# A gated mix of two long convolutions: P rows in two buffers, one reader per PSUM tile, and a new written-out order

## The chip, the cores and the metric

The kernel runs on one core of one Trainium2 chip. The metric is the device time of one execution in microseconds (us), lower is better. Several runs of the kernel are timed, and their median stands for it. The profile is taken from one further execution.

The engines are named as in the profile: PE is TensorE (matrix products into PSUM), PEld its loading of weights, DVE is VectorE, ACT is ScalarE, POOL is GpSimd and SP is SyncE. SP issues most transfers, POOL and ACT some.

## The reference

Both branches take the same input x (1 x 2048 x 448, bf16). Branch A is a long convolution of x with a kernel K that is built from 256 complex modes for each of 448 channels; branch B convolves a 4-tap convolution of k, times v, with a given kernel ssm_k, and multiplies by x. A gate for each time step mixes them:

```
g = sigmoid((x * gate_w).sum(-1, keepdims=True))
# A
logdA = exp(log_dt)[:, None] * (A_re + 1j * A_im)
P = exp(logdA[:, :, None] * l[None, None, :])          # 448 x 256 x 2048, complex
K = einsum("dn,dnl,dn->dl", C, P, dt * B).real
a = irfft(rfft(pad(x)) * rfft(pad(K)))[:2048] + x * Dskip
# B
kv = shift_conv(k, shift_k) * v                        # 4 taps
b = x * (irfft(rfft(pad(kv)) * rfft(pad(ssm_k)))[:2048] + kv * ssm_D)
return g * a + (1 - g) * b
```

## The kernel before, in words

**Layout.** The 448 channels are 4 groups of 112. The work is cut into four chunks H of 28 channels per group (NQG = 4, NC = 28), and each chunk of K into two blocks j (NBLK = 8 blocks of CB = 14 channels per group, M = 112 channels in a block over both halves of the modes and all groups).

**The long convolutions** are transforms by matrix products. For one chunk of one signal, spread_in multiplies the columns by Wc into PSUM tiles (ps_c in the profile), which ScalarE copies to a tile zs; transform multiplies by W2 (s_W in the profile; PSUM tile ps) and copies back; swapped makes a second tile zsS with the two halves of the partitions exchanged, by DMA; products multiplies the two by the transform of the other signal on VectorE. Stage a multiplies by R (sa_R; PSUM tiles ps_a, result U) and stage b by G (sb_G; PSUM tiles ps_b), and an epilogue takes ps_b. These tiles of 7168 bytes in each partition (zs, zsS, zsK, U, some of the early ones) share a ring with the tag "q" of NBQ = 7 buffers: a new tile takes the buffer of the one seven before it, and its first writer waits for that one's last reader.

**The kernel K** (class KGen, line 408) is a product of two tables of powers, Q rows (32, tile kg_TQ, for two blocks at once: q_rows, line 426) and P rows (32, tile kg_TP, for one block), multiplied by TensorE into a PSUM bank pk (224 matmuls for a block). Both come from ET (EQ and EP), powers at a few levels, by products of complex numbers on VectorE: mult (line 414) writes four products into a tile kg_P4 (kg_P in the profile), add (line 423) sums them in pairs. In block (line 458) the first 8 of the leading 16 P rows are made so. Rows 8 to 15 are two multiplications, one into kg_P4 and one into rows 8 to 15 themselves, and a DMA from GpSimd's queue that adds the first onto the second (accum_op). back then makes the 16 mirrored rows from the leading 16 in two instructions (128x1792), rows 8 to 15 of the mirrored ones first: kg_TP <- kg_TP, ET in the profile. ScalarE copies pk to S (kg_S), and gather (line 502) sorts S into KT (kg_KT) by matmuls with selecting matrices (PSUM tiles ps_g); spread puts KT into the tile zsK of the chunk (KA).

**The exponents** (class Tables, line 542): the products dt * A (real and imaginary) and the coefficients B * C stand in one tile hold for each half of the modes, with three planes for each block; save (line 595) writes what later chunks need to DRAM in two DMAs, and levels (line 611) loads them for chunk H. For each level VectorE makes a phase (ks_ph), ScalarE its sine (ET <- ks_ph) and the exponential of the real part (ks_mag), VectorE multiplies them; ScalarE makes a negated copy of parts of EQ (ET <- ET), 12 instructions in all. Sine and exponential need different tables on ScalarE, loaded by an ACT_TABLE_LOAD at each change between them.

**The other operations the change touches.** sk_cols (line 738) adds ssm_D to the first column of ssm_k's chunk on GpSimd, ahead of spread_in. transform_half (line 354) transforms half a chunk's zsK at the end: two PSUM tiles of two banks, 16 matmuls each, with two copies by two engines (evac_two, line 715, lets ScalarE and VectorE alternate).

**The sequence.** body (line 675) does the setup and the first chunk of B, then step (line 939) for blocks 0 to 6, each with one chunk of A or B; then the tail (lines 988 to 1009): the last chunk of A's signal, B's last chunk, block 7, mix (line 924), and the halves of the last convolution.

**The order.** All these calls are not issued where they stand: the class Order records them with numbers, and issue (line 148) lays them out as the string ORDER (lines 42 to 111) lists them, with a dependency from each instruction to the one before it on the same engine. So each engine's order is written out by hand, every instruction has the line L148 in the profile, and groups are told apart by tile names.

Of the kernel before, what the change touches and what calls it, by code (L numbers as in the profile page):

```python
# [10 lines left out]
ALU = mybir.AluOpType  # L11
f32 = mybir.dt.float32
# [5 lines left out]
P = 128  # L18
# [8 lines left out]
M = 8 * CB  # L27
# [11 lines left out]
NBQ = 7  # L39
# [3 lines left out]
    "0-1 540 2 945 947 23 886 559 533 553-554 896-897 560 31 13 544 538 542-543 967 36 946 539 546 549 60 12 551 22 "  # L43
    "561 563 565 569 955 562 8 970 566 61 953-954 25 62-68 572-580 831 934 931 928 529 3 930 938 7 564 53 34-35 557 "
    "601-605 568 606-609 32 582-589 33 30 531 962 541 545 548 581 4 9 17 29 936 958 591 914 905 44 889 907 550 887 "
    "941 590 874 851 878 527-528 11 555 850 864 968 956 926 833 556 619-623 929 830 592-599 860 863 924 855 28 927 "
    "829 600 843 859 836 835 834 610-614 14 24 839 948 898-899 949 877 530 942 842 837 950 832 933 838 27 615-617 "
    "932 923 957 879 16 624-627 618 854 847 873 960 861 963 875 628 865 868 26 20 70 41 848 631 535 844-845 18 880 "
    "567 532 840 849 906 964 69 630 470-497 19 937 629 299-326 925 888 883 558 959 876 852-853 916 185-212 915 866 "
    "856-857 965 858 890 869-870 547 891 882 862 867 908 1500 498-525 42 900 570 871 917 885 918 872 327-354 841 971 "  # L50
    "213-240 43 961 966 881 355 55 552 241 10 15 5 21 6 951 526 356-411 58 939 534 536 38 242-297 884 128-155 57 56 "
    "943 412 909 846 39 952 537 298 2873 2887 2883 40 571 2884 46 413-440 1478 2885 441-469 2896 37 54 632 935 "
    "156-184 2888 71-98 2895 2877 99-127 910 892 921 913 2878 911 2876 940 912 1480 47 684-692 893 920 903 650-666 "
    "633-648 667-679 919 680-682 649 683 765-771 895 772-781 1479 2882 48 45 748-764 711-719 731-737 720-727 738-746 "
    "728 782-789 894 969 747 1151-1164 790 1483 1165-1166 901 904 1125-1140 1486 922 1481 1167 902 49 51 1142-1150 "
    "1141 791-799 693-701 1491 1202-1209 702-710 944 1108-1124 1482 2874 1502 1210 1168-1181 1501 1182-1183 "
    "1091-1103 1484 1503 1104-1106 52 50 1184-1191 1107 809-816 1489 1192-1200 817 800-807 1201 59 972-1001 1504 "
    "1271-1278 808 1002-1016 1279 1490 1505 2875 1298-1305 1487 1017-1031 1306 1506 1032-1046 1493 1307-1315 1507 "
    "1047-1061 818-826 1494 1508 1062-1084 2880 1316-1323 1495 729 1085-1086 1324 1492 2563-2569 1325-1333 2570-2578 "
    "1496 2579 1485 1883-1890 1499 1891 1849-1862 1488 1498 1476 1497 2879 1510 1863-1864 2881 1334-1342 730 2889 "  # L60
    "1509 1511 1280-1287 1289-1296 1512-1543 1865 1297 2897 1544-1639 1473 828 1640-1703 2900 1704-1735 1288 2899 "
    "2901 827 2118-2119 2904 1736 2905-2906 2120 1245-1261 2909 2121 2908 2910 2919 2122 2918 2123 1228-1244 "
    "1262-1269 2892 1270 2920 2124 2886 1211-1218 1474 2893 2126 1475 2125 2890 1219-1227 2911 2128 1477 2922 "
    "2537-2544 1755-1794 2545 2902 2520-2535 1795 1408-1439 2907 2536 2486-2502 2898 2894 2503-2519 2903 1440-1455 "
    "1828 1456-1471 2923 1737-1753 2924 1343-1358 2912 2921 1359-1390 2914 2913 1391-1406 1472 2127 1754 1866-1872 "
    "2915 2891 1829 2946 2928 2927 2129 2937 1814-1821 2969 2943 1873-1879 2938 2934-2935 2933 2666-2673 2929 2674 "
    "2916-2917 2940 1407 2930 1880-1882 2925 2130-2161 1831 2162-2193 1830 2194-2225 1832-1845 2675-2682 1846-1848 "
    "2683 2947 2944 2226-2353 2948 2971 1909-1916 1822 2949 2932 1823-1826 2354 2926 2970 1827 1952-1960 2945 2941 "
    "1805-1812 1943-1951 2693-2701 1917-1925 2931 2952 1892-1907 1926-1941 2942 2972 1813 1942 2936 2955 1908 "
    "2546-2552 2973 2553-2561 4620-4626 2958 2974 1796-1803 2959 4627-4628 2684-2691 2597-2604 2975 2939 2562 2605 "  # L70
    "1804 2692 2580-2595 2962 2950 2373-2413 1961-1968 1970-1977 2596 1969 1978 2711-2718 2355-2371 2702-2709 2719 "
    "4145 4153 2720-2727 2963 2951 2961 2053-2068 2710 2069-2116 2964 2976 2965 2372 2977 2728 2979 4149 2729-2737 "
    "2432-2439 4152 2440 2968 2953 1988-2019 2966 4148 4151 4147 2960 2954 2020-2035 4186 4150 3298 2117 2423-2431 "
    "2956 2967 2036-2051 2978 3318-3324 2980 4146 2957 4176 3352-3359 4154 3360 2981-3044 4177 3587 4185 4187 3297 "
    "3045-3076 3300 3299 2441-2444 3077-3108 4167 2445 4178 2870 3325-3334 4168 1979-1987 4169 2414-2422 3109-3172 "
    "4160 4159 4161 3173-3205 2466-2473 2052 4180 3589 3588 2474 3361-3368 4165 4164 4166 3412-3420 3590 3395-3402 "
    "4181-4182 3591 4170 4155 3592-3593 3403-3410 3369-3376 3378-3385 3411 3386-3393 3377 2457-2464 3394 4156-4157 "
    "3301-3314 4191 4190 3335-3341 2446 3342-3350 3315-3316 2465 3224-3263 4192 3594-3595 3522-3553 3317 3554-3569 "
    "4200 3570-3585 3351 4162 2475-2482 3597 3264 4158 4179 2483 4193 4188 3596 4195 4194 4196 3457-3488 3206-3222 "
    "3586 3223 3489-3520 4163 4171 3274-3281 4172-4173 2448-2455 4183 4199 3282 5892-5899 3283-3290 4197 2456 3598 "  # L80
    "5900 4205 4203 1087 4204 4209 4212 3599-3630 3430-3437 2447 4184 4218 3521 4213 3631-3662 2868 4202 2871 4241 "
    "3421-3428 3663-3726 4215 4174 4214 4175 3727-3822 4216 3429 3823 4217 2869 2485 2484 2640-2647 4201 3291 4211 "
    "3438 4242-4243 3292-3295 2648-2655 3296 4219 2656 4220-4221 2657-2665 4244 4206 4224 3265-3272 4245 3439-3447 "
    "4198 2623-2639 4227 2606-2613 4210 3273 4189 4208 4222 3448-3455 4246 4207 5415 4223 2872 5050-5062 4247 4230 "
    "4249 3842-3882 4226 3824-3840 4248 4250 3456 2614-2621 4233 3841 3901-3908 4231 4225 5063-5065 4234 2622 5066 "
    "5442 4586-4592 5067-5079 4235 5080-5082 3909 5083 4593-4602 2803-2834 5441 5422 5424 5423 5093-5099 4232 4251 "
    "4236 2835-2866 1088 4237 5417 2738-2769 4228 5421 4240 4229 2867 5429 5419-5420 5100-5108 4239 3915 2770-2801 "
    "5127-5140 4252 5141-5142 5418 4238 4665 5109 5143 3892-3900 2802 5416 5084-5091 5443 5033-5048 3910-3913 "
    "5430-5431 5446-5447 5437-5438 4569-4575 3914 5432 5448-5449 5426 5439 4576-4584 5049 4253-4316 1090 4317-4444 "
    "5425 4445-4476 5455 5444 5427 5092 5222-5229 5434 5456 4667 5435 4585 5457 4666 5436 4668 5144-5150 4669 5458 "  # L90
    "5151 4670-4671 3883-3890 4672-4673 5230 5875-5881 5470 5882-5890 5450 4675 5451 5152 3891 3917-3924 3944-3951 "
    "5891 5110-5123 4477 5469 3952 1089 5124-5125 3925 5126 5472 5428 5471 5461 3926-3934 5452-5453 5240-5247 "
    "3935-3942 4478-4494 5213-5220 3943 5221 5460 5462 4603-4616 5248 5440 5276-5283 5464 4617-4618 5231-5238 5454 "
    "5511 5465 3916 5463 5459 5433 4674 4676-4772 3954 5466 5445 5489 5467 4495 5476 5284 4773-4804 5482 5239 "
    "4805-4836 5487 4837-4868 3953 4869-4900 5490 4619 3972-3987 5491 5512 5494 5513 5478 5473 4496-4535 3989-3996 "
    "5497 5481 5492 3997-4004 5468 3988 3955-3962 4005-4013 3963-3970 4536 5493 4014 4656-4663 5514 5499 5837 "
    "4546-4553 5496 5515 5500 5498 5484 3971 4554 4664 5841-5854 5516 5258-5266 5855-5856 5501 5838 4564-4568 "
    "5267-5275 5475 4555-4563 4629-4637 4901 5517 4638-4645 5504 4537-4544 5488 4080-4095 4545 4646 4096-4111 "
    "4920-4960 5519 5485 4902-4918 5505 5483 5518 5858-5871 4919 4970-4977 5872-5873 5857 5506 4978 5474 5480 5486 "
    "4112-4143 5477 4015-4030 5502 4961-4969 4144 5507 5479 4031-4078 4979-4986 4079 5495 4987 5503 5510 5249-5256 "  # L100
# [251 lines left out]


def transform_half(nc, psum, W, zs, evac, half):
    for kk in range(2):
        pt = psum.tile([P, 2, 512], f32, name="ps_2", tag="ps")
        for i in range(16):
            k = 16 * kk + i
# [686 lines left out]
```

## Time and profile before

| | before |
|---|---|
| median of 3 runs | 277.68 us (277.12 to 280.39) |
| profiled execution | 277.69 us, of which the span is 275.8 us |
| TensorE: matmuls, weight loads | 210.7 us (76% of the span), 193.3 us (70%) |
| VectorE | 241.7 us (88%), 488 instructions |
| ScalarE | 226.7 us (82%), 383 instructions |
| GpSimd | 15.9 us (6%), 51 instructions |
| mean granted TensorE clock | 0.956 |
| accumulate DMA kg_TP <- kg_P | 8 issues of 448 KB, 5.7 us to landing (median) |
| ScalarE's table loads | 11, 1283 ns each |

How to read it: the span is the profiled stretch from the first instruction to the last, and 1.9 us of the execution lie around it. A row for a group of instructions gives its engine, operation, output <- inputs, shape and count, then its busy time and the mean of one, then how long the engine was idle just ahead of them and what ended that. A row of the waits gives the waiting engine and tile, what it waited for, and the total, number and longest of the waits. A row of the timeline gives start, duration, and in brackets the idle time before it. Instructions of one engine overlap somewhat, so that the time from start to start is shorter than the duration.

### The profile page before, as it was taken

The page shows a single profiled execution, that of the slowest core. Times are in us where ns is not written, and L with a number is a line of the kernel's source. Part 1 is how long each engine was busy: PE and PEld are TensorE (multiplying, and loading weights), DVE is VectorE, ACT ScalarE, POOL GpSimd, SP SyncE. Part 2 cuts the span into 40 slices and gives each one's busy share as a digit, 9 for nine tenths or more (in the row PEclk, how much of TensorE's full clock was granted, in tenths as well). Part 3 has the DMA queues.
Part 4 walks back from the last instruction along what each step waited for, and adds up shares of the span by engine and source line. Part 5 has one row for each costly group of instructions (what it writes and reads, how often), then busy time and mean ns, then how long its engine had stood idle before and what let it go on. Part 6 is the DMA issues. An engine that isn't in the chain of part 4 may idle for free.

```text
span 275.8 us, 12739 instructions
## 1 busy us (share of the span) xinstructions
PE 210.7 (76%) x5770; PEld 193.3 (70%) x5770; DVE 241.7 (88%) x488; ACT 226.7 (82%) x383; POOL 15.9 (6%) x51
## 2 busy tenths in 40 slices
PE   0610958879988799798997789867887999699830
PEld 0500858877887798687995779766886899688820
DVE  7599899999989799979996899899999997967950
ACT  2795696999899999998998799999999989546400
POOL 8000000000400000100010001001001001000000
PEclk9999999999999899998998999999999999979975
DMA  7999799607804500390093019003042263600077
GB/s 149 224 204 172 131 235 175 99 1 153 118 5 91 116 5 4 83 186 5 5 209 47 5 50 199 10 2 70 6 90 64 54 138 60 147 5 2 2 141 127
DMA packets 55110, 24.74 MB, mean 90 GB/s; under 512 B 49680, under 2 KB 52368, under 8 KB 55056
## 3 DMA queue, kind: packets, MB, share of 16 engines
q1 hardware_dynamic: 48640, 19.34, 37.7%
q0 software_dynamic: 1152, 3.67, 7.2%
q10 hardware_dynamic: 5264, 0.92, 2.1%
q8 instruction: 45, 0.74, 1.2%
q14 instruction: 9, 0.07, 0.1%
HBM read 7.95 MB, written 2.87 MB: 39 GB/s over the span
## 4 chain that ended last, share of the span: by engine, by line
ACT 38%; PE 29%; DVE 15%; DMA 9%; issue 5%; SPq 0%; DVEq 0%; POOL 0%; POOLq 0%; ACTq 0%
ACT zs L148 15%; ACT ET L148 7%; ACT U L148 6%; DMA kg_TP<-kg_P 6%; PE pk L148 5%; PE ps_a L148 5%; PE ps L148 5%; PE ps_c L148 5%; PE ps_b L148 5%; ACT zsK L148 5%; DVE vt L148 2%; DVE scratch L148 2%; PE ps_g L148 2%; PE ps_gate L148 2%; DMA skraw<-in_B_ssm_k_dram 2%
## 5 line engine op out<-in xcount | busy, mean ns | idle before, releaser
L148 ACT CAST zs<-ps 128x896 bf16<-128x896 f32 x48 | 44.0, 944 | 1.0 <-PE ps L148 0.6
L148 ACT CAST zs<-ps_c 128x1024 bf16<-128x1024 f32 (+1 forms) x48 | 42.7, 937 | 1.3 <-PE ps_c L148 1.2
L148 PEld LDWEIGHTS <-front 128*32 128x32 bf16 (+1 forms) x496 | 19.1, 159 | 27.3 <-issue 22.3
L148 PEld LDWEIGHTS <-s_W 128*128 128x128 bf16 x544 | 28.9, 100 | 12.7 <-issue 9.6
L148 PE MATMUL pk<-kg_TP,kg_TQ 128*32 128x32 bf16 x1792 | 33.2, 242 | 5.1 <-issue 2.9
L148 PEld LDWEIGHTS <-kg_TQ 128*32 128x32 bf16 x1792 | 31.2, 160 | 7.0 <-issue 4.8
L148 PE MATMUL ps_a<-sa_R,zs 128*128 128x128 bf16 x224 | 32.7, 235 | 0.3
L148 ACT CAST U<-ps_a 128x1024 bf16<-128x1024 f32 (+1 forms) x30 | 27.2, 936 | 6.9 <-PE ps_a L148 6.7
L148 PE MATMUL ps_b<-U,sb_G 128*128 128x28 bf16 x1024 | 29.5, 175 | 4.1 <-issue 1.4
L148 PE MATMUL ps_a<-sa_R,zsS 128*128 128x128 bf16 x224 | 32.1, 232 | 0.5 <-DVE zsS L148 0.5
L148 PE MATMUL ps<-zs,s_W 128*128 128x112 bf16 x384 | 27.7, 220 | 5.5 <-ACT zs L148 4.2
L148 PEld LDWEIGHTS <-sb_G 128*128 128x128 bf16 x1024 | 27.8, 96 | 5.8 <-issue 3.2
L148 DVE TENSOR_TENSOR kg_TP<-kg_TP,ET 128x1792 bf16<-128x1792 bf16 x24 | 26.1, 1090 | 5.8 <-DMA kg_TP<-kg_P 5.0
L148 PEld LDWEIGHTS <-zsS 128*128 128x128 bf16 x224 | 29.6, 152 | 1.3 <-DVE zsS L148 0.7
L148 PEld LDWEIGHTS <-zs 128*128 128x128 bf16 x224 | 29.4, 151 | 0.8
L148 PE MATMUL ps_v<-front 128*32 128x336 bf16 (+3 forms) x448 | 16.0, 310 | 16.0 <-DVE front L148 13.1
L148 ACT ACTIVATE ET<-ks_ph 128x448 bf16<-128x448 int16 x40 | 23.2, 602 | 4.1 <-DVE kg_P L148 2.6
L148 DVE TENSOR_TENSOR kg_TQ<-kg_TQ,ET 128x896 bf16<-128x896 bf16 (+1 forms) x36 | 24.8, 730 | 0.0
L148 DVE TENSOR_TENSOR kg_P<-kg_TP,ET 128x1792 bf16<-128x1792 bf16 (+1 forms) x24 | 22.4, 934 | 0.1
L148 PE MATMUL ps_c<-Wc,uu 128*64 128x128 bf16 x224 | 18.4, 290 | 1.6 <-ACT U L148 0.6
L148 PE MATMUL ps_c<-Wc,vt 128*64 128x128 bf16 x224 | 17.1, 285 | 1.4 <-ACT zs L148 1.2
L148 PEld LDWEIGHTS <-uu 128*64 128x64 bf16 x224 | 16.5, 210 | 2.4 <-issue 1.5
(102 smaller groups left out, 427.4 us busy)
## 6 DMA issues: line engine op xcount, KB each, us to landing
zsS<-zs SPq DMA_DIRECT2D x16, 448.0 KB, 5.7
kg_TP<-kg_P POOLq DMA_DIRECT2D x8, 448.0 KB, 5.7
vt<-in_B_v_dram SPq DMA_DIRECT2D x4, 448.0 KB, 6.8
skraw<-in_B_ssm_k_dram SPq DMA_DIRECT2D x16, 112.0 KB, 4.8
uu<-in_A_u_dram SPq DMA_DIRECT2D x4, 448.0 KB, 8.5
ks_xf<-xfd SPq DMA_DIRECT2D x3, 336.0 KB, 3.3
out_dram<-vt ACTq DMA_DIRECT2D x8, 112.0 KB, 3.8
out_dram<-vt SPq DMA_DIRECT2D x8, 112.0 KB, 3.6
```

Source lines behind the costliest of these rows:

```text
L148: ins = f(*args, **kw)
```

## The change: what it does, and the diff

- **P rows.** One tile TA of 48 rows is allocated once in place of a tile of 32 rows for each block. Even blocks have their leading 16 rows at 0 to 15, odd ones at 32 to 47, and the mirrored rows of both are 16 to 31. TensorE's operand for pk spans the mirrored rows and the block's own leading ones; for odd blocks the halves come in the other sequence, so that S is rotated by 16 rows, and gather splits selections that wrap around (16 matmuls more in all). The tile is 7168 bytes a partition larger, and NBQ goes from 7 to 6.
- **Rows 8 to 15 of block 7** are made by two mult and add pairs of four rows each in place of the two multiplications and the accumulate DMA. The other blocks keep the DMA (in a function summed).
- **Exponents and coefficients** are held in three separate parts for each half of the modes in place of three planes of one tile; save writes six DMAs in place of two.
- **The 12 negations of Q** go from ScalarE to VectorE, the 4 additions of sk_cols from GpSimd to VectorE.
- **transform_half** uses four PSUM tiles of one bank, 8 matmuls and one copy each.
- **ORDER** is new throughout. The number of recorded calls goes from 6758 to 6779.

```diff
-NBQ = 7
+NBQ = 6
...
 def transform_half(nc, psum, W, zs, evac, half):
-    for kk in range(2):
-        pt = psum.tile([P, 2, 512], f32, name="ps_2", tag="ps")
-        for i in range(16):
-            k = 16 * kk + i
-            nc.tensor.matmul(pt[:, i // 8, (i % 8) * 56:(i % 8 + 1) * 56], lhsT=W[:, k].rearrange("p r s -> p (r s)"),
-                             rhs=half_of(zs, k, k + 1, half), start=True, stop=True)
-        for i in range(2):
-            k0 = 16 * kk + 8 * i
-            evac(half_of(zs, k0, k0 + 8, half), pt[:, i, 0:448].rearrange("p (k c) -> p k c", c=CB), i)
+    for kk in range(4):
+        pt = psum.tile([P, 512], f32, name="ps_2", tag="ps")
+        for i in range(8):
+            nc.tensor.matmul(pt[:, i * 56:(i + 1) * 56], lhsT=W[:, 8 * kk + i].rearrange("p r s -> p (r s)"),
+                             rhs=half_of(zs, 8 * kk + i, 8 * kk + i + 1, half), start=True, stop=True)
+        evac(half_of(zs, 8 * kk, 8 * kk + 8, half), pt[:, 0:448].rearrange("p (k c) -> p k c", c=CB), kk % 2)
...
+    def summed(self, dst, src, r, m):
+        n = src.shape[1]
+        part = self.pool.tile([P, 8 * 2 * M], bf16, name="kg_P4", tag="kg_P4", bufs=2)[:, 0:n * 2 * m]
+        for c, out in enumerate((part.rearrange("p (n v m) -> p n v m", n=n, v=2), dst)):
+            self.nc.vector.tensor_tensor(out=out, in0=src[:, :, c].unsqueeze(2).to_broadcast([P, n, 2, m]),
+                                         in1=bass.AP(r.tensor, r.offset + c * m, [list(r.ap[0]), [0, n], [-m, 2], [1, m]]), op=ALU.mult)
+        self.nc.gpsimd.dma_start(dst.rearrange("p n v m -> p (n v m)"), part, accum_op=ALU.add)
...
-        TP = self.pool.tile([P, 32, 2, M], bf16, name="kg_TP")
+        if j == 0:
+            self.TA = self.pool.tile([P, 48, 2, M], bf16, name="kg_TP")
+        TP, late = self.TA[:, 32 * (j % 2):32 * (j % 2) + 16], self.TA[:, 16:32]
+        both = self.TA[:, 16 * (j % 2):16 * (j % 2) + 32]
...
-            V.tensor_tensor(out=TP[:, 16 + i0:16 + i1], in0=src,
+            V.tensor_tensor(out=late[:, i0:i1], in0=src,
...
+        if j == NBLK - 1:
+            add(8, mult(TP[:, 0:4], 64))
+            add(12, mult(TP[:, 4:8], 64))
+        else:
+            self.summed(TP[:, 8:16], TP[:, 0:8], EP[:, entry_of(64) - EQ_N + 1], M)
...
-                        r0 = TP[:, 0, c, m:m + 1]
-                        rhs = bass.AP(r0.tensor, r0.offset, [list(r0.ap[0]), [32 * M + (1 - 2 * c) * M, 2], [2 * M, 16]])
+                        d = c ^ (j % 2)
+                        r0 = both[:, 0, d, m:m + 1]
+                        rhs = bass.AP(r0.tensor, r0.offset, [list(r0.ap[0]), [32 * M + (1 - 2 * d) * M, 2], [2 * M, 16]])
...
-        self.hold = [early[:, 4096 + 1344 * i:5440 + 1344 * i].bitcast(f32).rearrange("p (b t m) -> p b t m", b=4, t=3) for i in range(2)]
+        part = lambda i, t: early[:, 4096 + 1344 * i + 448 * t:4544 + 1344 * i + 448 * t].bitcast(f32).rearrange("p (b m) -> p b m", b=4)
+        self.hold = [[part(i, t) for t in range(3)] for i in range(2)]
...
-            self.dma.dma_start(self.xfd[:, 4 * i + b:4 * i + 4], t[:, b:4])
+            for k in range(3):
+                self.dma.dma_start(self.xfd[:, 4 * i + b:4 * i + 4, k], t[k][:, b:4])
...
-                    nc.scalar.mul(B[:, :, 2], B[:, :, 0], -1.0)
+                    V.tensor_scalar(out=B[:, :, 2], in0=B[:, :, 0], scalar1=-1.0, scalar2=None, op0=ALU.mult)
...
-        nc.gpsimd.tensor_tensor(out=raw[:, :, 0], in0=raw[:, :, 0], in1=dB[:, H * NC:(H + 1) * NC], op=ALU.add)
+        V.tensor_tensor(out=raw[:, :, 0], in0=raw[:, :, 0], in1=dB[:, H * NC:(H + 1) * NC], op=ALU.add)
```

## The prediction, made before the changed kernel ran

> **What bounds the kernel now.** I read the totals and the chain first, then the waits of VectorE, the windows, and the last 40 us instruction by instruction.
>
> ```profile
> span 275.8 us, 12739 instructions
> PE 210.7 (76%) x5770; PEld 193.3 (70%) x5770; DVE 241.7 (88%) x488; ACT 226.7 (82%) x383; POOL 15.9 (6%) x51
> ACT 38%; PE 29%; DVE 15%; DMA 9%; issue 5%; SPq 0%; DVEq 0%; POOL 0%; POOLq 0%; ACTq 0%
> ```
>
> VectorE (DVE) has the longest list, and the chain of work that ended last passes between ScalarE (ACT), TensorE (PE) and VectorE: no engine alone sets the end. The windows say where each does:
>
> ```profile
> 140.00:160.00 20.00, 16.47 (x507) 14.89 (x494) 16.70 (x34) 17.11 (x35) 1.01 (x2) 0.91 0.36 67
> 160.00:180.00 20.00, 17.27 (x553) 16.15 (x553) 19.14 (x39) 19.73 (x36) 0.86 (x1) 1.00 0.40 89
> 180.00:200.00 20.00, 15.79 (x471) 14.53 (x464) 18.99 (x42) 19.97 (x33) 0.85 (x1) 1.00 0.14 27
> 200.00:220.00 20.00, 16.98 (x444) 15.39 (x435) 19.50 (x32) 19.86 (x38) 0.85 (x1) 1.00 0.34 72
> 240.00:250.00 10.00, 9.80 (x314) 8.92 (x307) 6.56 (x9) 3.96 (x7) 0.00 (x0) 0.83 0.02 5
> ```
>
> (Stretch, length, busy time of PE, weight loads, VectorE, ScalarE, GpSimd, clock, DMA.) From 140 to 160 both VectorE and ScalarE sit idle for some 3 us; from 160 to 220 ScalarE is 99% busy and VectorE 96%; from 240 to 250 TensorE is the bound. VectorE's waits:
>
> ```profile
> DVE kg_TP L148 <- DMA kg_TP<-kg_P: 5.0, 3, 2.1
> DVE kg_KT L148 <- PE ps_g L148: 3.4, 1, 3.4
> DVE ks_ph L148 <- ACT ET L148: 3.1, 5, 1.1
> DVE ks_ph L148 <- ACT early L148: 3.0, 1, 3.0
> DVE zsS L148 <- ACT zsK L148: 2.7, 2, 1.9
> DVE kg_TP L148 <- PE pk L148: 1.4, 2, 0.8
> ```
>
> The first is the accumulate DMA ahead of the mirrored rows; the sixth is P rows that may not be overwritten before pk's matmuls have read the last block's.
>
> **The sum's base.** The profiled execution took 277.69 us for a span of 275.8; the median of the three runs is 277.68, so both are the same base. All terms below are on VectorE's path up to the last row of block 7, then on the tail's path behind that row.
>
> **VectorE gets work: +2.7.** Twelve negations come from ScalarE. The like row is 274 ns an instruction (TENSOR_SCALAR ET<-ET, 128x448), 0.19 us from start to start (158.61 to 158.80): 8 x 0.19 and 4 half as wide at 0.13 make 2.0; by full durations it is 3.0 at most, and 0 if they fill idle time. Four sk adds from GpSimd are 28 elements a lane; the nearest row (128x64, start to start 148.36 to 148.52) gives 0.16, I take 0.1 each, 0.4. Block 7 has two adds in place of its DMA: 128x896, 0.62 us each, 0.54 start to start, 1.1. That is 3.5 in all. Over the new list up to and with the last row instruction, the same durations sum to 220.3 where they summed to 217.6: 2.7, the rest of the 3.5 is offset by work now listed behind it. No cover is claimed.
>
> **Waits for P rows go: -6.4.** With two buffers the leading rows of a block are written while TensorE still reads the other block's: the 1.4 goes, since the mirrored rows shared by both come last in a block. The accumulate DMA takes 5.7 us from issue to landing (median; 4.3 to 8.2) and in the new list has 7 to 18 us of VectorE work between its multiplications and its reader, where it had about 5: the 5.0 goes. What is late next is ScalarE's activation for ks_ph, below. If that cover shrank to the old 5 us, the old rate would come back, 5.0 over 8 DMAs, 0.6 for each of the 7 left, 4.4; if a DMA took the longest landing, 8.2, the shortest cover falls short by 1.2.
>
> **ScalarE gets lighter: -2.0.** Twelve negations cost it 5.1 + 1.8 us of rows:
>
> ```profile
> L148 ACT ACTIVATE ET<-ET 128x448 bf16<-128x448 bf16 x8 | 5.1, 638 | 1.0 <-DVE ET L148 1.0
> L148 ACT ACTIVATE ET<-ET 128x224 bf16<-128x224 bf16 x4 | 1.8, 440 | 0.0
> L148 ACT ACT_TABLE_LOAD x11 | 14.1, 1283 | 2.9 <-issue 2.8
> ```
>
> The new order alternates Sin and Exp more often in the first chunk: 15 loads where there were 11, all four more ahead of the first zs cast. ScalarE's list ahead of that cast goes from 33.4 to 37.8 us, its list behind it from 193.3 to 189.0 (nine negations, 5.2, less 0.9 of copies now behind the cast), so -4.3 where it is saturated. VectorE's waits on it for ks_ph (3.05) then shrink; I take 2.0, between 0 (ScalarE stays behind) and 3.05.
>
> **The start: -0.5.** Ahead of the first zs cast ScalarE has 48.0 - 33.4 = 14.6 us of idle time, so four loads (4 x 1.28 = 5.1) fit:
>
> ```profile
> 45.58 1.28 ACT L148 ACT_TABLE_LOAD   x1
> 46.88 0.39 ACT L148 ACTIVATE ET<-early 128x224 bf16<-128x224 f32 x1
> 48.01 2.39 ACT L148 CAST zs<-ps_c 128x512 bf16<-128x512 f32 x3
> ```
>
> The activation starts 0.02 us after its load's end: a switch costs 1.3. The Trainium skill, "ScalarE: Activation LUTs", section What ACT_TABLE_LOAD costs, adds a drain of about 1380 ns to the 1283 ns load; by an estimate from it the four switches are 10.6 us and the list ahead of the cast ends near 37.8 + 9 x 1.38 = 50.2, which would delay the first cast by 2.2 and give 272.7. The row shows no such gap.
>
> Splitting exponents from coefficients takes a false wait apart (3.0, ks_ph <- ACT early) and one of ScalarE (2.4, ET <- early). Before 48 us many things overlap, and the first ps_v matmuls wait 13.1 for VectorE anyway; I take 0.5 off, from +1.5 (the loads in the way) to -5.4 (both waits whole). SP gets 4 more DMA issues in save, about 0.4 us each, ahead of loads that are needed tens of us later; hidden, 1.6 if not. GpSimd loses its four adds, whose 45.8 us of waiting held only its own queue: 0.
>
> **Six buffers for seven: +0.5.** In the new list a q buffer is reused at least 25 places of its engine after its last reader, but for two: the KA tile (zsK) of chunk 1 (4 places) and that of chunk 3 (3). The second waits for ps_a matmuls that stand within pk of block 7. I take 0.25 each; 0 if the readers are done, and about 2 each if each waits as the largest like row does, 1.9 (zsS <- zsK).
>
> **Last row to kg_S: -2.2.** The path before:
>
> ```profile
> 235.69 1.09 DVE L148 TENSOR_TENSOR kg_TP<-kg_TP,ET 128x1792 bf16<-128x1792 bf16 x1
> 237.06 0.46 PE L148 MATMUL pk<-kg_TP,kg_TQ 128*32 128x32 bf16 x16
> 239.63 2.04 PE L148 MATMUL pk<-kg_TP,kg_TQ 128*32 128x32 bf16 x112 [2.11 <-issue]
> 244.43 1.75 PE L148 MATMUL pk<-kg_TP,kg_TQ 128*32 128x32 bf16 x96
> 246.35 0.56 ACT L148 CAST kg_S<-pk 128x448 bf16<-128x448 f32 x1
> 253.57 0.54 ACT L148 CAST zsK<-ps 128x448 bf16<-128x448 f32 x1 [1.52 <-DVE zsK L148]
> ```
>
> Rows end at 236.8, kg_S at 246.9: 10.1. The new list has 224 pk (0.46 + 2.04 + 1.75 = 4.25) with 16 ps_a matmuls between (24 took 2.8 at the lower clock of 242 us, so 1.9 by that, 1.1 at the 0.066 us from start to start of 246 us; I take 1.2, since one long stretch ends nearer to the latter) in one stretch, 1.3 of TensorE's queue that is still ahead when the rows are done, the cast 0.56 and 0.6 of handing over: 7.9. It is 10.1 again if the 2.11 of "issue" and the places of the rest come back for another cause than the list.
>
> **Behind kg_S: +1.5 - 0.8.** TensorE's list behind kg_S goes from 17.1 to 18.6 us: ps_2 and ps_b matmuls of half 0 now stand there (1.1 and 1.8), others stand ahead, and the gather's split gives 4 more matmuls here (0.06 each) and 12 in other blocks (0.7, TensorE has idle time there). The tail is TensorE's (98% busy from 240 to 250), so +1.5; 0 if ScalarE and VectorE set its pace, 2.9 if nothing moved ahead. One reader per PSUM tile takes away half of the 1.52 wait of the cast at 253.57 for VectorE's: -0.8, from 0 to -1.5.
>
> Sum: -0.5 + 2.7 - 6.4 - 2.0 + 0.5 - 2.2 + 1.5 - 0.8 = -7.2, so 277.7 - 7.2 = 270.5.
>
> **The rivals.** *ScalarE keeps the pace.* At 99% busy from 160 to 220, VectorE's waits could be filled without effect, as they'd move to waits for casts. Then only ScalarE's own list counts: -4.3 and +0.5 for the buffers, 273.9. For it: the chain has 38% on ScalarE. Against it: between 140 and 160 it idles too, at the very waits that go.
>
> *Six buffers make every allocation wait; slower.* After the first products 31 tiles (zs, zsS, zsK, U) are allocated in that ring. Seven were tight: of the casts into a fresh buffer four started 0.1, 0.3, 0.4 and 0.7 us after its release. If each of the 31 holds a saturated engine up by d, 7.7 is cancelled at d = 0.25; at d = 0.43 the time is 283.2, at 0.47 284.5, which is the time I give it. Against it: the distance of 25 places, some 12 us of VectorE or ScalarE work, is larger than any wait on the list.
>
> *The split does not do what it says.* If TensorE's reads and VectorE's writes of the two buffers are still held apart as one tile, the 1.4 stays and the extra buffer brings nothing: 271.9. It lies in the forecast's range.
>
> *A drain at each switch*, as weighed above: 272.7.
>
> **How the numbers follow.** The forecast and its near cases (270.5, own range 264 to 272.1) get 0.54; ScalarE's pace (273.9) 0.18; the drain 0.02; buffers that cost between 0.25 and 0.43 each 0.08; buffers at 284.5 0.18. Two per cent, about what a measurement of this kernel tells from no change, is 5.55 us: faster ends at 272.1, slower begins at 283.2. So faster 0.54, same 0.28, slower 0.18. The low end takes the start's -5.4 for -0.5, the whole 3.05 of ks_ph and no buffer wait: 270.5 - 4.9 - 1.05 - 0.5 = 264.0. The high end is 283.0, where the fourth case ends; with the last case outside, 2 in 10 are left out.
>
> **What would show it.** Right: no kg_TP <- DMA and no kg_TP <- PE pk among VectorE's waits; 15 table loads, the first zs cast still near 48; ET<-ET on VectorE x20 and none on ScalarE; VectorE near 245 busy; kg_S of block 7 near 239, and a span near 268.6. Wrong: waits of ScalarE or VectorE for q buffers (zs, U or zsS <- PE) of several us in all; a first zs cast after 50; VectorE's idle time moved from kg_TP to ps_b, ps_c or ks_ph with the total as before; a stretch from kg_S to the end much above 29.

## The result, and the profile after

| | before | after |
|---|---|---|
| median | 278.75 us (4 runs, 277.12 to 280.39) | 267.34 us (4 runs, 266.37 to 269.04) |
| ratio | 1 | 0.960, 95% interval 0.951 to 0.968 |
| profiled execution, its span | 277.69, 275.8 | 266.88, 264.8 |
| VectorE, ScalarE, TensorE busy | 241.7, 226.7, 210.7 | 243.4, 226.8, 213.7 |

The kernel is 4.0% faster; 270.5 was forecast, 264 to 283. The gain is 11.4 us by the medians and 11.0 by the two profiles, where the sum had 7.2. Executions more than 1.5% above the fastest of their kernel are left out of the ratios and times below: four of ten of b_neg_vec (279.8 with them), one of ten of b_late and two of four of b_dve_load.

The busy times did not fall; idle time went, 12.7 us on VectorE and 11.1 on ScalarE. The head of the page after:

```profile
span 264.8 us, 12775 instructions
PE 213.7 (81%) x5786; PEld 194.2 (73%) x5786; DVE 243.4 (92%) x506; ACT 226.8 (86%) x375; POOL 11.8 (4%) x46
DVE 37%; ACT 35%; PE 16%; DMA 4%; issue 3%; SPq 0%; ACTq 0%; DVEq 0%
```

The chain's share of TensorE went from 29% to 16%, of DMA from 9% to 4%. Three rows of the windows after, with columns as before, answer to the middle and the tail; the last line is one window of 160 us.

```profile
140.00:160.00 20.00, 18.40 (x559) 16.57 (x559) 19.96 (x42) 19.79 (x40) 0.85 (x1) 1.00 0.40 90
160.00:180.00 20.00, 18.34 (x524) 17.13 (x520) 19.19 (x36) 19.97 (x34) 0.86 (x1) 1.00 0.23 50
240.00:250.00 10.00, 8.71 (x241) 8.48 (x240) 9.55 (x14) 5.75 (x7) 0.00 (x0) 1.00 0.01 3
...
60.00:220.00 160.00, 149.44 (x4070) 135.46 (x4069) 156.60 (x296) 156.61 (x267) 6.17 (x7) 0.96 0.36 73
```

VectorE and ScalarE are each busy for 98% of the time from 60 to 220 us, TensorE for 93%. The kernel before, in the same window:

```profile
60.00:220.00 160.00, 138.89 (x3840) 126.45 (x3841) 149.44 (x280) 153.05 (x267) 8.33 (x9) 0.97 0.34 68
```

Where VectorE waits now:

```profile
DVE front L149 <- DMA scratch<-in_B_shift_k_dram: 3.1, 1, 3.1
DVE ks_ph L149 <- ACT ET L149: 1.9, 2, 1.1
DVE vt L149 <- PE ps_v L149: 1.2, 2, 1.1
...
DVE zsS L149 <- ACT zsK L149: 0.6, 2, 0.4
DVE kg_KT L149 <- PE ps_g L149: 0.6, 1, 0.6
```

kg_TP waits neither for its DMA (5.0) nor for pk (1.4) any more. Three instants of the timeline split the gain; the sums of busy and idle time between them are taken from VectorE's timeline.

| | before | after | forecast for the step |
|---|---|---|---|
| last P row written | 236.8 | 228.4 (-8.4) | -5.7 |
| of this, VectorE busy / idle | 217.6 / 19.2 | 218.3 / 10.1 | +2.7 / -8.4 |
| from the last P row to the end of kg_S | 10.1 | 6.65 (-3.45) | -2.2 |
| from the end of kg_S to the end of the span | 28.9 | 29.8 (+0.9) | +0.7 |

### The profile page after: what moved, and what is told of

It reads as the page before. It is cut to its first block, busy times and chain, and to the rows that moved or that the text cites. A ratio compares the mean times of both kernels' runs of the same rounds, so it can differ in the third digit from the quotient of the medians.

```text
span 264.8 us, 12775 instructions
## 1 busy us (share of the span) xinstructions
PE 213.7 (81%) x5786; PEld 194.2 (73%) x5786; DVE 243.4 (92%) x506; ACT 226.8 (86%) x375; POOL 11.8 (4%) x46
## 4 chain that ended last, share of the span: by engine, by line
DVE 37%; ACT 35%; PE 16%; DMA 4%; issue 3%; SPq 0%; ACTq 0%; DVEq 0%
ACT zs L149 12%; ACT zsK L149 7%; ACT ET L149 6%; DVE kg_P L149 5%; PE ps_v L149 4%; ACT U L149 4%; DVE kg_TQ L149 3%; PE ps_b L149 3%; DVE kg_TP L149 3%; DVE ET L149 3%; PE ps_c L149 3%; DVE zsS L149 3%; DVE vt L149 3%; DVE zs L149 3%; DVE sb_G L149 2%
## 5 line engine op out<-in xcount | busy, mean ns | idle before, releaser
L149 ACT CAST zs<-ps_c 128x1024 bf16<-128x1024 f32 (+1 forms) x48 | 44.0, 976 | 0.5 <-PE ps_c L149 0.4
L149 PEld LDWEIGHTS <-front 128*32 128x32 bf16 (+1 forms) x496 | 19.9, 160 | 27.8 <-issue 17.3
L149 PE MATMUL pk<-kg_TP,kg_TQ 128*32 128x32 bf16 x1792 | 35.4, 241 | 0.9 <-issue 0.7
L149 PEld LDWEIGHTS <-s_W 128*128 128x128 bf16 x544 | 27.9, 98 | 7.9 <-issue 4.5
L149 PE MATMUL ps_b<-U,sb_G 128*128 128x28 bf16 x1024 | 30.8, 178 | 2.6 <-DVE U L149 1.2
L149 PEld LDWEIGHTS <-sb_G 128*128 128x128 bf16 x1024 | 28.7, 98 | 4.7 <-issue 1.9
L149 PE MATMUL ps_v<-front 128*32 128x336 bf16 (+3 forms) x448 | 17.3, 319 | 17.1 <-DVE sb_offs L149 6.9
L149 PE MATMUL ps_a<-sa_R,zsS 128*128 128x128 bf16 x224 | 31.1, 227 | 0.0
L149 DVE TENSOR_TENSOR kg_TP<-kg_TP,ET 128x1792 bf16<-128x1792 bf16 x23 | 24.7, 1083 | 0.5 <-ACT ET L149 0.5
L149 DVE TENSOR_TENSOR kg_P<-kg_TP,ET 128x1792 bf16<-128x1792 bf16 (+1 forms) x25 | 23.3, 934 | 0.1
L149 ACT ACT_TABLE_LOAD x15 | 19.2, 1283 | 2.0 <-issue 1.8
```

The costliest lines, as they stand in the source:

```text
L149: ins = f(*args, **kw)
```

## The experiments

Each is a kernel after with something undone or added (names with a_), or the kernel before with something put in (b_). Medians are compared with 267.3 (after) and with the runs of the kernel before beside them (277.4 to 277.9); ratios are to the latter. The kernel after was timed with the result alone, where the kernel before took 278.75, so a difference of about 1 us from 267.3 tells nothing.

**a_neg_act: negations back on ScalarE.**

```diff
-                    V.tensor_scalar(out=B[:, :, 2], in0=B[:, :, 0], scalar1=-1.0, scalar2=None, op0=ALU.mult)
+                    nc.scalar.mul(B[:, :, 2], B[:, :, 0], -1.0)
```

> The changed kernel with one part undone: the 12 negations of Q are back on ScalarE, at the same places of the order. In the changed kernel, between the first zs cast and the last P row (48.4 to 228.4), VectorE is idle for 3.8 us and ScalarE for 4.6 us. Theory A (both engines are near their bound, what counts is which list is longer in a stretch): VectorE's list loses 2.0 us, ScalarE's gains 5.2 behind the cast, 0.6 more than it has idle time, so ScalarE is the bound again and VectorE's waits for ks_ph come back: 268 to 271 us against 267. Rival (ScalarE alone sets the pace): the whole 5.2, 272. Rival (the negations are no part of the gain, it is all order and P rows, and VectorE alone is the bound): VectorE's 2.0 come off, 265.

Measured: 276.2 us, ratio 0.995 (0.992 to 0.999): +8.9, more than any theory gave. The longest of VectorE's waits is new:

```profile
DVE kg_P L149 <- ACT ET L149: 8.3, 5, 3.1
```

The first products of the Q rows (kg_P) read the negated copies. In the new order they stand close behind the levels on VectorE's list. With the copy on ScalarE, VectorE waits five times until ScalarE has come to it in its own queue, and between the first zs cast and the last P row it idles for 12.5 us where it idled for 3.8; the first zs cast is 3.2 us later as well (in a profiled execution of 277.7 us).

**b_neg_vec: negations on VectorE, alone.** The same line the other way, in the kernel before.

> The kernel before with one part of the change alone: the 12 negations on VectorE, nothing else, in the order of before. Theory A (as in the prediction: +2.0 on VectorE's list against 2.0 of its waits for ScalarE that go): about 278, from 276.5 to 279.5. Rival (ScalarE sets the pace from 160 us on): -4 to -5, 273 to 274. Rival (VectorE's list alone counts): +2.0, 280.

Measured: 278.9 us, ratio 1.003 (0.9994 to 1.0067), so -0.2 to +1.9 us. This lies in theory A's range; ScalarE as the pace (-4 to -5) is out for the old order, and VectorE's list alone (+2.0) lies just above the interval, too near to be called out. That +2 and -2 balance is not shown either: in its profile, of an execution of 281.4 us, the waits for ks_ph that were to go are still there (3.1 before):

```profile
DVE ks_ph L148 <- ACT ET L148: 2.9, 5, 1.1
```

So a part that is worth little or nothing there holds up 8.9 us in the new order.

**a_act_load and a_dve_load: is it the length of the list or the wait?** A tile dum that nothing reads, and behind each negation:

```diff
+                    dum = self.dum[:, 0:n * 2 * M].rearrange("p (n m) -> p n m", n=n)
+                    nc.scalar.mul(dum, B[:, :, 0], -1.0)
```

or, in a_dve_load, two `V.tensor_tensor(out=dum, in0=B[:, :, 0], in1=B[:, :, 0], op=ALU.mult)`.

> The changed kernel with 12 activations more on ScalarE, one behind each negation, of the negation's size (8 of 638 ns, 4 of 440 ns by the rows of before, 6.9 us in all, some 5.2 of it behind the first zs cast), into a tile that nothing reads; the negations stay on VectorE, so VectorE waits for none of them. Theory H (putting the negations back on ScalarE cost 9 us mostly since VectorE then waits for their results, 8.3 us by its waits, and not by ScalarE's longer list): ScalarE has 4.6 us of idle time in the middle, so +1 to +4: 268 to 271 us. Rival L (ScalarE's list is what cost the 9 us): +7 to +9, 274 to 276.

> The changed kernel with 24 multiplications more on VectorE, two behind each negation, of its size (387 ns for 448 elements by the rows of before, 0.31 from start to start; about 6.6 us in all, 5 of it behind the first zs cast), into a tile that nothing reads. Theory H (in the new order VectorE has 3.8 us of idle time in 180 and everything waits for it): the whole 5 to 7 us, 272 to 274 us, or more, as three waits of 11.4 us in all cost 15.6. Rival (ScalarE is as near its bound, so part of it falls into time in which VectorE would have waited): +1 to +3.

Measured: a_act_load 271.0 (+3.7), ratio 0.978 (0.973 to 0.982); a_dve_load 272.4 (+5.1), ratio 0.981 (0.976 to 0.986). The added activations took 6.5 us of ScalarE:

```profile
L149 ACT ACTIVATE dum<-ET 128x448 bf16<-128x448 bf16 x8 | 4.8, 597 | 2.4 <-DVE ET L149 2.4
L149 ACT ACTIVATE dum<-ET 128x224 bf16<-128x224 bf16 x4 | 1.7, 416 | 0.0
```

The same load on ScalarE costs 3.7 when nobody waits for it and 8.9 when VectorE does, although VectorE is 2 us lighter in the second case. Theory H holds: the larger part of a_neg_act is the round trip, not the list. On VectorE the added loads, 7.1 us of busy time by the last P row, cost 5.1.

**b_act_load and b_dve_load: the same loads in the kernel before.**

> The kernel before with the same 12 activations more on ScalarE, behind its own negations, read by nothing. ScalarE has 8.4 us of idle time between the first zs cast and the last P row there. Theory H (in the order before no engine's list sets the end; waits go round between the engines): +1 to +4, 279 to 282 us. Rival (ScalarE, 99% busy from 160 to 220 us, sets the pace): +5 to +7, 283 to 285.

> The kernel before with the same 24 multiplications more on VectorE, two behind each of ScalarE's negations, read by nothing. VectorE has 13.3 us of idle time in the middle there. Theory H (VectorE's waits of before are slack: taking 2.9 us of them away brought nothing): 0 to +3, 278 to 281 us, and VectorE's idle time in the middle goes from 13.3 to about 9. Rival (VectorE's list counts in full, as the prediction's sum took it): +5 to +7, 283 to 285.

Measured: b_act_load 280.6 against 277.4, ratio 1.012 (1.007 to 1.018): +3.2, as H expected. b_dve_load: 281.6 and 282.3, ratio 1.016 (1.009 to 1.023), +4.5, from two executions. This lies between H and its rival. Its profile says where: ahead of the first zs cast +3.5; from there to the last P row only +1.6 for 5.7 us of added busy time, since VectorE's idle time fell from 13.3 to 9.3 us. In a_dve_load the same stretch grew by 3.6 for 5.2 added, and its idle time fell only from 3.8 to 2.2. So by one profile each the old order had slack on VectorE in the middle and the new one has little; ahead of 48 us both have little. The totals do not tell the orders apart: the loads cost 3.2 and 4.5 in the old one, 3.7 and 5.1 in the new.

**b_late: the P rows' DMA gets more cover in the old order.** On VectorE's list the mirrored rows of blocks 1 and 2 that need the DMA stand 1.8 and 1.4 us of work later; no other edit.

> The kernel before with the cover of two accumulate DMAs made longer and nothing else: on VectorE's list the mirrored rows that need the DMA are moved behind 1.8 us of other work in block 1 and behind 1.4 us in block 2, where VectorE waited 1.41 and 1.49 us. Theory A (a VectorE wait that goes shortens the time by its length): -2.5 to -2.9, 275 us. Rival (from 80 to 135 us the waits are filled by other waits, since ScalarE is 96% busy there): within 0.7 of 278.

Measured: 277.8 against 277.9, ratio 0.999 (0.995 to 1.003), so at most 1.3 us gained: theory A falls. The waits, in an execution of 276.3 us:

```profile
DVE kg_TP L148 <- DMA kg_TP<-kg_P: 2.3, 2, 1.7
DVE kg_TQ L148 <- PE pk L148: 1.3, 1, 1.3
DVE kg_P L148 <- ACT ET L148: 1.1, 1, 1.1
```

The wait for the DMA fell from 5.0 to 2.3, as intended, but two waits that weren't there came, for TensorE and ScalarE, 2.4 together. Here waits that were taken away alone came back as waits for other engines.

**a_hoist: the cover taken away in the new order.** On VectorE's list the mirrored rows of blocks 0, 2 and 5 come 6 to 12 places earlier, right behind the last multiplication.

> The changed kernel with the cover of three accumulate DMAs taken away: in blocks 0, 2 and 5 the mirrored rows that need the DMA come right behind the ones that don't and the last multiplication, as the first thing on VectorE. Landings are 4.4, 4.2 and 4.2 us there and 0 to 1.0 us of work is left ahead: waits of about 3.4 to 4.4 us each, 11 in all. Theory A (VectorE's waits in the middle cost their length, as it has 3.8 us of idle time in 180): +9 to +11, 276 to 278 us against 267. Rival (TensorE gets the rows 6 us earlier and ScalarE sets the pace, so most of the waits are absorbed): +1 to +4, 268 to 271.

Measured: 282.9 us, ratio 1.017 (1.009 to 1.024): +15.5, more than the waits themselves and than theory A's +11:

```profile
DVE kg_TP L149 <- DMA kg_TP<-kg_P: 11.4, 3, 5.2
DVE front L149 <- DMA scratch<-in_B_shift_k_dram: 2.9, 1, 2.9
DVE ks_ph L149 <- ACT ET L149: 1.7, 2, 1.0
DVE ET L149 <- ACT ET L149: 1.6, 1, 1.6
DVE kg_TP L149 <- PE pk L149: 1.5, 1, 1.5
```

ScalarE then waited in turn for VectorE, and VectorE's idle time in the middle went from 3.8 to 19.6 us. The rival (TensorE gains by the early rows) is out. The granted clock was lower too, 0.91 to 0.92 where the kernel after had 0.94 to 0.97, and TensorE was busy 2.8 us longer in the middle; what share of the 15.5 that has is not told apart.

**b_parts: the parts without the order.** The kernel before, with its order, its one P tile and its seven buffers, and these parts: negations and sk additions on VectorE, block 7's four instructions in place of the DMA, exponents and coefficients apart, gather's 16 matmuls more.

> The kernel before, in its own order and with its seven buffers and its one P tile, with these parts of the change: negations and the sk additions on VectorE, block 7's rows 8 to 15 by two mult and add pairs, exponents and coefficients apart with six save transfers, and the 16 added matmuls of gather (split without a rotation). Left out: the second P buffer, the sixth-buffer limit, the one reader per PSUM tile, and the new order. Theory A (these parts are about worth their prices: VectorE +3.5, ScalarE's waits -2.0, false waits of the start -0.5; the gain sits in the order that the second P buffer allows): +1, from 277 to 280.5 us. Rival (the parts carry the gain): 272 or less.

Measured: 282.6, ratio 1.014 (1.008 to 1.021): +4.6, 2 us above theory A's upper end, and against the rival. So these parts do not carry the gain; what is left, the new order with the second P buffer and the one reader per PSUM tile, has to bring 15 us over them. The order and the buffer belong together: in the new order 7 to 9 of a block's 11 P-row instructions on VectorE start ahead of the end of the pk matmuls of the block before, and the leading rows of one buffer may not be overwritten until these have read them. Neither was tried alone, so how the 15 us divide is not shown; nor is it whether the old order would run as well with six buffers.

**a_dma7: block 7 with the DMA again.**

```diff
-        if j == NBLK - 1:
-            add(8, mult(TP[:, 0:4], 64))
-            add(12, mult(TP[:, 4:8], 64))
-        else:
+        if True:
             self.summed(TP[:, 8:16], TP[:, 0:8], EP[:, entry_of(64) - EQ_N + 1], M)
```

> The changed kernel with rows 8 to 15 of block 7 made as in the other blocks: two multiplications and the accumulate DMA in place of the two mult and add pairs; the DMA is issued where the two multiplications end. Theory A (VectorE's list up to the last P row sets the end, and the products zsS and zs, 4.0 us, with the mirrored rows that do not need the DMA, 1.0, cover a landing of 4.3): two adds go, 1.1 less, 266 us against 267. Rival (the DMA's landing of 4.3 to 5.7 behind its issue is not covered): VectorE waits 0.5 to 2 us for it, 267 to 268, and the adds were the right choice.

Measured: 270.2, ratio 0.973 (0.967 to 0.979): +2.9. Neither theory: VectorE did not wait for the DMA, and the last P row came at 226.3, 2.1 earlier. TensorE gained nothing by it, since its own queue brings it to these pk matmuls at 228.9 in this kernel and at 229.0 after, and then it paused:

```profile
228.91 1.22 PE L148 MATMUL pk<-kg_TP,kg_TQ 128*32 128x32 bf16 x64
232.34 0.72 PE L148 MATMUL pk<-kg_TP,kg_TQ 128*32 128x32 bf16 x32 [2.21 <-issue]
...
234.96 2.34 PE L148 MATMUL pk<-kg_TP,kg_TQ 128*32 128x32 bf16 x128
```

The kernel before has a pause of 2.11 us at the like place, and the kernel after has none, though a swap zsS<-zs was in flight at that time in all three. Of the fourteen kernels profiled, the six that make block 7's rows with the DMA all pause in these matmuls, for 1.2 to 2.2 us, and the eight that do not, b_parts in the old order among them, do not.

The traces say more of the pause. In all fourteen, counting TensorE's matmuls, weight loads and waits in the order of the trace, every pause over 0.5 us that is put down to issue (36) stands where another 256 of them begin. And a queue that the page calls instruction moves 45 pieces of 16 KB, here in the kernel before, one for every 256 of its 11,540 matmuls and weight loads:

```profile
q8 instruction: 45, 0.74, 1.2%
```

At the boundary ahead of the pause, a pair of swaps had been issued 1.4 us earlier in the kernel before and 0.9 us earlier in a_dma7, and the next piece began to move 3.5 and 3.8 us behind the boundary. In the kernel after the swaps were 0.5 us old there, and the piece began after 0.4 us. So the pause looks like TensorE waiting for its next instructions behind the swaps, and whether it comes seems to hang on a part of a microsecond. No run varied this alone.

**a_two_readers: one part undone.** transform_half as before.

> The changed kernel with transform_half as before: two PSUM tiles of two banks, 16 matmuls each, read by two copies, in the second half by two engines; every engine's order stays. Theory A (the prediction's step): a copy of ScalarE waits for VectorE's copy of the same tile and back, 0.75 us each time, once or twice in the tail: +0.8 to +1.5, 268 to 269 us. Rival (these waits were the false order of one run and lie beside TensorE's work): within 0.3 of 267. Rival (a tile of two banks is held longer, and TensorE waits for a PSUM buffer as well): +2 or more.

Measured: 268.3, ratio 0.968 (0.960 to 0.975): +1.0, with intervals that overlap. Its profile has kg_S within 0.5 us of the kernel after and the stretch from kg_S to VectorE's last instruction at 21.5 for 20.3. That agrees with theory A's +0.8 to +1.5 in size, by one profile, and not in kind: no copy of ScalarE waits for one of VectorE there, while TensorE's waits for ScalarE's copies (ps <- ACT zsK) in the tail are 0.9 us where they were 0.2.

**a_wraw: three loads earlier.** On ScalarE's queue the loads of shift_k stand ahead of the first activation.

> The changed kernel with one thing moved: the three loads of shift_k on ScalarE's queue that stand behind its first activation (which waits for another load until 4.4 us) are issued ahead of it. In the changed kernel VectorE waits 3.1 us for the last of them at 9.3 us. Theory A (VectorE's list sets the end from the start on, 42.2 of the first 48.4 us are busy): -2 to -3.1, 264 to 265 us, and the first zs cast comes 2 to 3 us earlier. Rival (ahead of 48 us the transfers of k and v, or ScalarE's table loads, set the pace, and VectorE's gain is lost again in a later wait of the start): within 0.5 of 267, with the first zs cast at 48.

Measured: 266.9, ratio 0.962 (0.955 to 0.968): no difference, and the first zs cast at 48.3. VectorE's 3.1 us wait shrank to 0.9 and came back elsewhere in the start (1.8 for ScalarE where 0.4 stood, 0.6 for early). The rival holds: the start is not VectorE's.

## Why the prediction was right, and where its sum was not

**Direction and cause.** The waits for P rows (-6.4) are gone, and VectorE's idle time up to the last P row fell by 9.1 where -8.4 was forecast (-0.5 -6.4 -2.0 +0.5). The mechanism was right: two buffers and the order together take VectorE's waits away, and little comes in their place. The 1.4 for pk went too, so the two buffers are not held apart as one tile. How much is the buffer's and how much the order's stays open.

**What a wait is worth was wrong.** The sum took each wait at its length. b_late shows that 2.7 us of the same waits taken away in the old order are worth nothing, or 1.3 at most, and a_hoist that 11.4 put into the new one cost 15.5. That the sum came within 3.8 us of the 11.0 is in part luck: the new order took the waits of all three engines away together (TensorE idles 12.4 us in the middle for 23.5, ScalarE 4.6 for 8.4), which no term foresaw; as a list of independent terms it was not valid.

**The cover of the DMA** was said to be 7 to 18 us for about 5. By the timeline it is 6.1 to 11.8 for 5.3 to 8.3 in blocks 0 to 6. The other half is the landing, which the prediction took as unchanged:

```profile
zsS<-zs SPq DMA_DIRECT2D x16, 448.0 KB, 4.4
kg_TP<-kg_P POOLq DMA_DIRECT2D x7, 448.0 KB, 4.4
```

The medians were 5.7 and 5.7. Before, the DMAs of blocks 2, 3 and 4 were issued 1.1 to 2.8 us behind a pair of swaps and landed after 8.2, 7.5 and 6.9 us; the first of them:

```profile
115.13 1.11 SPq L148 DMA_DIRECT2D zsS<-zs  x2
116.41 1.44 SPq L148 DMA_DIRECT2D skraw<-in_B_ssm_k_dram  x1
```

(its issue stands at 116.21 on GpSimd). After, none is issued within 4.8 us behind a swap, and all land after 4.2 to 5.7. The rule is not sharp: block 1's before, issued 2.9 us behind the second swap of a pair, landed after 6.2. That the transfers slow each other is read from these times; no run varied it alone.

**ScalarE gets lighter (-2.0)** was the worst term in kind. VectorE's wait for ks_ph went from 3.1 to 1.9, so -1.2 by that row. But what moving the negations does in the new order is to spare VectorE a round trip of 8.3 us, which the prediction did not see, since the trace of before has no such wait: there the readers stand far behind.

**VectorE's list (+2.7)** was +0.7. The prices were right:

```profile
L149 DVE TENSOR_SCALAR ET<-ET 128x448 bf16<-128x448 bf16 x16 | 4.3, 270 | 0.0
...
L149 DVE TENSOR_TENSOR skraw<-skraw,dB 128x28 bf16<-128x28 bf16 x4 | 1.1, 281 | 0.0
```

From start to start the negations add 2.0 (2.0 forecast) and the four additions 0.45 (0.4). Block 7 gave +0.8 for 1.1, and work moved across the last row took 0.8 off (uu, vt and the gate's behind it, one zs product ahead of it). The rest, 1.7, are unchanged instructions that take less time from start to start, the largest a single one: sb_ph beside GpSimd's iotas at 1.9 us took 1.26, and takes 0.54 in its new place.

**Last row to kg_S (-2.2)** was -3.45. The rows after:

```profile
229.00 1.74 PE L149 MATMUL pk<-kg_TP,kg_TQ 128*32 128x32 bf16 x96
...
232.06 2.35 PE L149 MATMUL pk<-kg_TP,kg_TQ 128*32 128x32 bf16 x128
```

The two runs of pk took 4.1 (4.25 forecast). Mis-sized were the 1.3 of queue and 0.6 of handing over: rows end at 228.4, and TensorE starts at 229.0, 0.6 for both. The 2.11 of issue did go; that it hangs on the order was a guess. a_dma7 shows that it can return in the new order, and b_parts takes 6.7 us for the same stretch in the old one, so this step is not the new order's.

**Behind kg_S** +0.7 was forecast and +0.9 measured; the one reader's share of -0.8 agrees with a_two_readers in size (+1.0 when undone, about what can be told).

**The start (-0.5)** was +0.4: two false waits went, and a wait of 3.1 for shift_k came, which a_wraw shows to be worth nothing. The four added table loads lie beside other work:

```profile
45.79 1.28 ACT L149 ACT_TABLE_LOAD   x1
47.09 0.68 ACT L149 ACTIVATE ET<-early 128x224 bf16<-128x224 f32 x2
47.67 0.37 ACT L149 ACTIVATE ks_mag<-ks_xf 128x224 bf16<-128x224 f32 x1
48.44 2.84 ACT L149 CAST zs<-ps_c 128x1024 bf16<-128x1024 f32 x3 [0.40 <-PE ps_c L149]
```

The first zs cast waits for TensorE, not for the loads. The drain that the Trainium skill, "ScalarE: Activation LUTs", section What ACT_TABLE_LOAD costs, adds to a load is not to be seen here either: the activation starts 0.02 us behind the load's end, and the cast came at 48.4, not near 50.2.

**The slower rival** (six buffers): no q buffer shows among the long waits of VectorE or ScalarE, and the 0.5 set aside for it is 0. The reuse distances of the prediction were read on the footing that a tile may take any buffer of the ring that has been released, where the section on the kernel says the one of seven tiles before; no run shows which it is.

## What to carry to other kernels

Where several engines are each over 90% busy with fixed orders, do not price a wait at its length: taken away alone it may move to another engine (2.7 us for nothing), put into a tight order it may cost more than itself (15.5 for 11.4). Ask of every result that crosses to another engine and back how close its reader stands; a 0.6 us instruction on the wrong engine cost 0.7 us a piece here, through its queue. A test for which of these one has is a load that nobody reads: if it costs less than the same load with a reader, the wait counts more than the list. And where TensorE pauses for nothing that the profile names, count its instructions before you credit the order with the pause.

## What the runs showed of the hardware

- An accumulate DMA of 448 KB from GpSimd's queue landed after 6.9 to 8.2 us in the three blocks where the first of a pair of swaps had been issued 1.1 to 2.8 us ahead of it, and after 4.2 to 6.2 us in the other blocks of the kernels before and after.
- A VectorE instruction of 0.54 us (128x512 int32) took 1.26 us once, while GpSimd ran its iotas.
- All 36 pauses of TensorE over 0.5 us that the fourteen profiles put down to issue, the longest 2.2 us, stand at every 256th of its instructions; the kernel before has four (5.2 us together), the kernel after one (0.9 us). Pieces of 16 KB come on the instruction queue at that rate.
